# Tile 24 of w_down in nine transfers of 64 to 2 partitions instead of one of 128

## The chip, the core and the metric

The kernel runs on one core of one Trainium2 chip. The metric is device time in microseconds (us), one launch of the whole program, the median of three runs. A lower number is better. Beside the times there is one profiled execution, whose trace is read in what follows.

## The reference

One token (`x`, 1024 numbers) goes through a decoder layer whose two branches run in parallel, and both are added to `x`:

```
xn = layernorm(x)
q  = xn @ wq                                 # 1024 x 4096
p  = softmax(q k^T / sqrt(128))              # the last 4096 keys, 4 key heads, 32 query heads
a  = (p v) @ wo                              # 4096 x 1024
h  = gelu(xn @ w_gate) * (xn @ w_up)         # 1024 x 3584 each
y  = x + a + h @ w_down                      # 3584 x 1024
```

All of it is float32. With a single token every weight and every cached key and value is read once and used for one multiply-add per number, so the kernel moves 94.4 MB from HBM to do matrix-vector products.

## The kernel before

All large inputs pass through one buffer, `ring`, of 176 KB on each of the 128 partitions. A table `pieces` lists what is loaded, in order, and where in the ring: wq in two pieces, the keys, values, w_gate and w_up in two each, wo in two, and w_down in eight. The function `pump` issues the transfer of the next piece as soon as its place in the ring is no longer in use, and `done` frees a place when the last instruction that reads the piece has been recorded. All these transfers are issued by SyncE (SP), through the helper `dma` (line 219 of the profile), so SP's queue has them in the order of the table, and SP waits there for the engines that still read the old piece.

w_down has 3584 rows. Partition p holds rows 28p to 28p+27, and tile t is the row 28p+t of every partition: 128 partitions by 1024 numbers, 4 KB on each partition, 512 KB in all. The eight pieces are the tiles 0 to 11, 12 to 19, 20 and 21, 22 and 23, and then 24, 25, 26 and 27 one by one. Tile 27 comes in two transfers of half its columns.

The last part of the program multiplies these tiles by the hidden vector `hz`. Some tiles go to VectorE (DVE, `multiply_add`, line 213), which keeps a sum per partition in `part`; the others go to TensorE (PE, line 158). At the very end the order is: tiles 20 to 23, then tile 24 on PE (into `sums`), then the fold of DVE's `part` on PE, then tile 25 on PE, an addition on DVE (`x_out`, line 189), tile 26 and the two halves of tile 27 on PE (into `acc`), and after each half an addition on DVE into `y` and two stores to HBM (`out_y`), one from SP and one from ScalarE.

Waits are found by a small recorder, the class `Program`. It notes which bytes each operation reads and writes. Every transfer has a lane of its own, that is a semaphore of its own, which has counted 16 when the transfer is complete (`op["rank"] = 16`). A compute instruction that reads a piece waits for 16 on that semaphore; PE's first matmul of tile 24 is one of them.

Of the kernel before, what the change touches and what calls it, by code (L numbers as in the profile page):

```python
# [24 lines left out]

RING = 176 * KB
SCRATCH = 1024
HEADS_A = [0, 2, 4, 6, 8, 10, 12, 14]
HEADS_B = [0, 2, 4, 6, 8, 10, 12, 14]
HID_A = [0, 2, 4, 6, 8]  # L30
# [5 lines left out]
class Program:  # L36

    def __init__(self, nc):  # L40
        self.nc = nc
        self.ops = []
        self.seen = {}
        self.engines = dict(pe=nc.tensor, dve=nc.vector, act=nc.scalar, pool=nc.gpsimd, sp=nc.sync)

    @staticmethod
# [5 lines left out]
        hi = lo + 1 + sum(abs(s) * (n - 1) for s, n in ap.ap[1:])  # L52
        return ap.tensor.name, p0, p0 + count, lo, hi

    def add(self, engine, emit, reads, writes, dma=False, tag=None):
        op = dict(engine=engine, emit=emit, dma=dma, needs={}, tag=tag, id=len(self.ops),
                  boxes=[self.box(a) for a in writes + reads])
        op["lane"] = f"dma{op['id']}" if dma else engine
        for writing, aps in ((False, reads), (True, writes)):
            for ap in aps:  # L60
                name, p0, p1, lo, hi = self.box(ap)
                for wrote, q0, q1, a, b, other in self.seen.get(name, ()):
                    if not (writing or wrote) or q0 >= p1 or p0 >= q1 or a >= hi or lo >= b:
                        continue
                    if other["lane"] == op["lane"] and (engine == "pe" or not wrote):
                        continue
                    lane = other["lane"]
                    op["needs"][lane] = max(op["needs"].get(lane, -1), other["id"])
        for writing, aps in ((False, reads), (True, writes)):
            for ap in aps:  # L70
                name, p0, p1, lo, hi = self.box(ap)
                kept = self.seen.setdefault(name, [])
                if writing:
                    kept[:] = [
                        k for k in kept
                        if not (p0 <= k[1] and k[2] <= p1 and lo <= k[3] and k[4] <= hi)
                    ]
                kept.append((writing, p0, p1, lo, hi, op))
        self.ops.append(op)
        return op  # L80

    def plan(self):
        known = {e: {} for e in self.engines}
        for op in self.ops:
            mine = known[op["engine"]]
            waits = []
            for lane, other in sorted(op["needs"].items(), key=lambda n: -n[1]):
                if mine.get(lane, -1) >= other:
                    continue
                waits.append(other)  # L90
                for k, v in self.ops[other]["after"].items():
                    mine[k] = max(mine.get(k, -1), v)
            op["waits"] = waits
            op["after"] = dict(mine)
            op["after"][op["lane"]] = op["id"]
        for op in self.ops:
            for other in op["waits"]:
                self.ops[other]["told"] = True
        counts = {}
        for op in self.ops:  # L100
            if op["dma"]:
                op["rank"] = 16
            elif op.get("told"):
                counts[op["engine"]] = counts.get(op["engine"], 0) + 1
                op["rank"] = counts[op["engine"]]
# [41 lines left out]
def decode_layer(nc, x, k_cache, v_cache, wq, wo, w_gate, w_up, w_down, out):  # L147
# [29 lines left out]
    def dve(call, reads, writes, engine="dve"):  # L177
        prog.add(engine, call, reads, writes)
# [9 lines left out]
    def add(o, a, b):  # L188
        dve(lambda e: e.tensor_add(o, a, b), [a, b], [o])  # L189
# [24 lines left out]
            [i, factor, other], [o],  # L214
        )

    def dma(engine, o, i, reads=(), writes=(), tag=None):
        return prog.add(
            engine, lambda e: e.dma_start(o, i), list(reads), list(writes), dma=True, tag=tag  # L219
        )  # L220

    ring = sbuf("ring", P, RING)
# [2 lines left out]
    def rows(w, a):  # L225
        return w[512 * a:512 * (a + 1), :].rearrange("(p r) n -> p (r n)", r=4)

    def heads_of(a):
        return wo[2048 * a:2048 * (a + 1), :].rearrange("(p t) n -> p (t n)", p=P)

    hidden_rows = w_down.rearrange("(p t) n -> p t n", p=P)
# [12 lines left out]
    def load(kind, i, at, size):  # L244
        slot = ring[:, at * KB:(at + size) * KB]
        held[kind, i] = slot
        if kind == "v":
            src = v_cache[0, 2 * i:2 * i + 2, SK - WIN:, :].rearrange("g (p j) d -> p g (j d)", p=P)
            dma("sp", slot.rearrange("p (g n) -> p g n", g=2), src, writes=[slot], tag=(kind, i))
        elif kind == "k":  # L250
            src = k_cache[0, 2 * i:2 * i + 2, SK - WIN:, :].rearrange("g (s j) d -> s g (j d)", g=2, j=64)
            dma("sp", slot, src, writes=[slot], tag=(kind, i))
        elif kind == "d":
            lo, hi = i
            halves = 2 if lo == TD - 1 else 1
            wide = slot.rearrange("p (t n) -> p t n", n=D)
            for half in range(halves):
                cols = slice(half * D // halves, (half + 1) * D // halves)
                dst = wide[:, :, cols]
                dma("sp", dst, hidden_rows[:, lo:hi, cols], writes=[dst], tag=(kind, i, half))  # L260
        else:
            src = {
                "q": lambda: rows(wq, i), "g": lambda: rows(w_gate, i), "u": lambda: rows(w_up, i),
                "o": lambda: heads_of(i),
            }[kind]()
            dma("sp", slot, src, writes=[slot], tag=(kind, i))
# [4 lines left out]
    def pump():  # L271
        while queue:
            kind, i, at, size = queue[0]
            if any(at < hi and lo < at + size for lo, hi in live.values()):
                return
            load(*queue.pop(0))
            live[kind, i] = (at, at + size)
# [12 lines left out]
    for k in range(2):  # L290
        dst = x_out[31 + 64 * k:33 + 64 * k, :, :]
# [316 lines left out]
    def head(t):  # L608
        return oz[:, 32 * t:32 * t + 64]
# [38 lines left out]
    def contract(kind, i, z, dve_tiles, rows):  # L648
        w = held[kind, i].rearrange("p (t n) -> p t n", n=D)
        count = w.shape[1]  # L650
        rest = [(z(t), w[:, t, :]) for t in range(count) if t not in dve_tiles]
        if rows:
            tiles_on_rows(rest)
        else:
            for pair in rest:
                tile_on_pe(*pair)
        for t in dve_tiles:
            tile_on_dve(z(t), w[:, t, :])
        done(kind, i)
# [38 lines left out]

    state["total"] = 2 * TO + 12 - len(HEADS_A + HEADS_B + HID_A)
    contract("o", 0, head, HEADS_A, True)  # L700
    contract("o", 1, lambda t: head(TO + t), HEADS_B, True)
    contract("d", (0, 12), column, HID_A, True)
    add(out_part, acc[:].rearrange("p a n -> p (a n)"), out_part)
    contract("d", (12, 20), lambda t: column(12 + t), HID_B, False)
    contract("d", (20, 22), lambda t: column(20 + t), HID_C, False)
    contract("d", (22, 24), lambda t: column(22 + t), HID_D, False)
    tile_on_pe(column(24), held["d", (24, 25)])
    tile_on_pe(unit[:], out_part)
    tile_on_pe(column(25), held["d", (25, 26)], True)
    add(x_out[:].rearrange("p f n -> p (f n)"), sums[:], x_out[:].rearrange("p f n -> p (f n)"))  # L710
    for half in range(2):
        half_on_pe(column(26), held["d", (26, 27)], half, True, False)
    stores = out.rearrange("a b (f c n) -> (a b) f c n", f=2, c=4)
    for half in range(2):
        half_on_pe(column(27), held["d", (27, 28)], half, False, True)
        add(y[:, half, :], acc[:, half, :P], x_out[:, half, :])
        for k, engine in enumerate(("sp", "act")):
            src = y[31 + 64 * k:33 + 64 * k, half, :]
            dma(
                engine, stores[0, half, 2 * k:2 * k + 2, :], src, reads=[src],  # L720
                tag=("out", half, k),
            )
# [25 lines left out]
```

## Time and profile before

| | |
|---|---|
| median of 3 runs | 226.78 us (226.62 to 226.94) |
| the profiled execution's own time | 226.83 us |
| its span in the trace | 225.5 us |
| bytes read from HBM | 94.38 MB, 419 GB/s over the span |
| DMA busy | 9 tenths or more of the 16 engines' time in nearly every fortieth of the span |
| DVE, PE, ACT busy | 64%, 39%, 12% of the span |

A busy share of DMA is the mean over the core's 16 DMA engines: 0.25 in a stretch can be four engines that work through it while twelve are idle. The share can lie a little over 1, since a packet's record overlaps the next one's. The chain of waits is the path that ended last, followed back from the last instruction. A wait for a transfer is shown there from its issue to its landing, so it contains the time in which the transfer stood behind earlier ones.

### The profile page before, as it was taken

The numbers are of one execution on the slowest core, as the hardware profiler recorded it, in microseconds if no ns is written. First come the engines' busy times: TensorE is split into PE (matmuls) and PEld (weight loads), VectorE is DVE, ScalarE is ACT, GpSimd is POOL, SyncE is SP. The second block draws the span as 40 slices with busy tenths as digits, with TensorE's granted clock in tenths as the row PEclk, the third lists the DMA queues.
The fourth block names the chain that finished last, engine by engine and source line by source line (L and its number), as shares of the span: only waits on it lengthen the run. The fifth ranks groups of instructions, "written<-read, shape, count | busy, mean of one in ns | idle before, by whom it ended". The sixth has DMA issues, their size and how long they took to land.

```text
span 225.5 us, 1396 instructions
## 1 busy us (share of the span) xinstructions
PE 87.5 (39%) x574; PEld 34.8 (15%) x574; DVE 143.2 (64%) x127; ACT 26.3 (12%) x45; POOL 0.7 (0%) x6
## 2 busy tenths in 40 slices
PE   1200000007699007989002537137339204408475
PEld 0100000006263002462000111011002001002131
DVE  7500998499727990000998699869538804938691
ACT  2000000004555001482000300200000000000000
POOL 1000000000000000000000000000000000000000
PEclk9999999999999755999755667857855855965889
DMA  9899899899989999999999998999999999999992
GB/s 373 372 395 535 372 395 535 349 405 478 468 349 426 465 401 503 427 397 471 427 397 392 433 509 387 478 391 491 419 395 488 419 395 413 427 439 442 382 405 111
DMA packets 3317, 94.46 MB, mean 419 GB/s; under 512 B 350, under 2 KB 366, under 8 KB 1008
## 3 DMA queue, kind: packets, MB, share of 16 engines
q1 hardware_dynamic: 3288, 94.38, 97.5%
q8 instruction: 4, 0.07, 0.1%
q10 hardware_dynamic: 24, 0.01, 0.0%
q14 instruction: 1, 0.01, 0.0%
HBM read 94.38 MB, written 0.00 MB: 419 GB/s over the span
## 4 chain that ended last, share of the span: by engine, by line
DMA 65%; DVE 26%; PE 7%; issue 1%; SPq 1%; DVEq 0%
DVE part L213 24%; DMA ring<-in_B_w_down 19%; DMA ring<-in_A_wq 18%; DMA ring<-in_B_w_gate 15%; DMA ring<-in_A_wo 13%; PE acc L158 3%; PE tp L163 2%; PE s_p L158 2%; DVE part L209 1%; SPq L219 1%; DVE rows_sb L186 0%; DVE part L189 0%; DVEq L118 0%; SPq L118 0%
## 5 line engine op out<-in xcount | busy, mean ns | idle before, releaser
L213 DVE SCALAR_TENSOR_TENSOR part<-ring,xz,part 128x3584 f32<-128x3584 f32 (+1 forms) x19 | 78.8, 4148 | 26.6 <-DMA ring<-in_B_w_gate 22.6
L163 PE MATMUL tp<-ident,ring 128*128 128x128 f32 x128 | 20.3, 303 | 44.4 <-DMA ring<-in_A_k_cache 42.8
L213 DVE SCALAR_TENSOR_TENSOR part<-ring,oz,part 128x1024 f32<-128x1024 f32 x15 | 19.3, 1285 | 9.9 <-DMA ring<-in_A_wo 9.4
L172 ACT ACTIVATE ring<-tp 128x512 f32<-128x512 f32 x32 | 18.1, 596 | 58.4 <-PE tp L163 58.0
L163 PEld LDWEIGHTS tp<-ident,ring 128*128 128x128 f32 x128 | 15.0, 152 | 51.2 <-DMA ring<-in_A_k_cache 42.9
L209 DVE TENSOR_SCALAR part<-ring,xz 128x3584 f32<-128x3584 f32 (+1 forms) x3 | 6.5, 2176 | 19.7 <-DMA ring<-in_A_wq 12.1
L158 PE MATMUL acc<-ring,oz 128*32 128x512 f32 x64 | 11.7, 899 | 16.8 <-DMA ring<-in_A_wo 16.8
L213 DVE SCALAR_TENSOR_TENSOR part<-ring,hz,part 128x1024 f32<-128x1024 f32 x10 | 12.8, 1285 | 6.1 <-DMA ring<-in_B_w_down 5.8
L158 PE MATMUL acc<-part,unit 128*32 128x448 f32 (+1 forms) x48 | 7.3, 742 | 22.3 <-DVE part L213 22.3
L158 PE MATMUL o_p<-ring,pT 128*32 128x512 f32 x64 | 11.0, 847 | 7.1 <-DMA ring<-in_A_v_cache 6.5
L158 PE MATMUL acc<-ring,hz 128*32 128x128 f32 (+1 forms) x60 | 8.0, 616 | 10.1 <-DMA ring<-in_B_w_down 10.1
L158 PE MATMUL s_p<-ring,qz 128*32 128x512 f32 x64 | 9.3, 598 | 0.0
L163 PE MATMUL tp<-ident,rows_sb 128*128 128x128 f32 x16 | 3.5, 361 | 12.0 <-ACT rows_sb L172 11.8
L158 PE MATMUL sums<-ring,hz 128*32 128x256 f32 x72 | 6.2, 482 | 4.7 <-DMA ring<-in_B_w_down 4.7
L158 PEld LDWEIGHTS acc<-ring,oz 128*32 128x32 f32 x64 | 2.5, 155 | 26.6 <-DMA ring<-in_A_wo 19.4
L158 PEld LDWEIGHTS acc<-part,unit 128*32 128x32 f32 x48 | 1.4, 126 | 26.4 <-DVE part L213 24.2
L172 ACT ACTIVATE rows_sb<-s_p,negm 128x512 f32<-128x512 f32 x2 | 1.4, 687 | 30.4 <-DVE negm L209 30.4
L158 PEld LDWEIGHTS o_p<-ring,pT 128*32 128x32 f32 x64 | 2.6, 149 | 14.5 <-issue 13.4
L158 PE MATMUL acc<-ring,xz 128*32 128x448 f32 x32 | 4.8, 767 | 0.0
L158 PEld LDWEIGHTS acc<-ring,hz 128*32 128x32 f32 x60 | 2.2, 135 | 15.8 <-issue 14.0
L163 PEld LDWEIGHTS tp<-ident,rows_sb 128*128 128x128 f32 x16 | 2.3, 179 | 15.5 <-ACT rows_sb L172 13.6
L158 PEld LDWEIGHTS sums<-ring,hz 128*32 128x32 f32 x72 | 2.4, 136 | 9.2 <-DMA ring<-in_B_w_down 7.3
(85 smaller groups left out, 47.8 us busy)
## 6 DMA issues: line engine op xcount, KB each, us to landing
ring<-in_B_w_gate SPq DMA_DIRECT2D x2, 7168.0 KB, 31.9
ring<-in_B_w_up SPq DMA_DIRECT2D x2, 7168.0 KB, 33.9
ring<-in_A_k_cache SPq DMA_DIRECT2D x2, 4096.0 KB, 39.7
ring<-in_A_v_cache SPq DMA_DIRECT2D x2, 4096.0 KB, 34.8
ring<-in_B_w_down SPq DMA_DIRECT2D x1, 6144.0 KB, 42.9
ring<-in_B_w_down SPq DMA_DIRECT2D x1, 4096.0 KB, 38.8
ring<-in_B_w_down SPq DMA_DIRECT2D x2, 1024.0 KB, 40.4
ring<-in_B_w_down SPq DMA_DIRECT2D x3, 512.0 KB, 42.0
```

What stands on the lines that cost most here:

```text
L158: "pe", lambda e: e.matmul(o, lhsT, rhs, start=start, stop=stop),
L163: prog.add("pe", lambda e: e.transpose(o, i, eye), [i, eye], [o])
L172: "act", lambda e: e.activation(o, i, func, scale=scale, **kw),
L209: dve(lambda e: e.tensor_scalar(o, i, s1, s2, op0=op0, **kw), reads, [o])
L213: lambda e: e.scalar_tensor_tensor(o, i, factor, other, op0=ALU.mult, op1=ALU.add),
L219: engine, lambda e: e.dma_start(o, i), list(reads), list(writes), dma=True, tag=tag
```

## The change

Tile 24 alone is loaded in another way. In place of one transfer of 128 partitions there are nine, of 64, 39, 5, 5, 5, 3, 3, 2 and 2 partitions, one after the other down the partitions. Each partition still receives its 4 KB of the same bytes at the same place. The nine share one lane and so one semaphore: `group` names the lane, each transfer adds 16 to `sizes`, and whoever waits for the tile waits for 9 x 16 = 144. Nothing else in the program is different.

```diff
+UNEVEN = 24
+SHARES = [64, 39, 5, 5, 5, 3, 3, 2, 2]
...
-    def add(self, engine, emit, reads, writes, dma=False, tag=None):
+    def add(self, engine, emit, reads, writes, dma=False, tag=None, group=None):
...
-        op["lane"] = f"dma{op['id']}" if dma else engine
+        op["lane"] = engine
+        if dma:
+            first = self.groups.setdefault(group, op["id"]) if group else op["id"]
+            op["lane"] = f"dma{first}"
+            self.sizes[op["lane"]] = self.sizes.get(op["lane"], 0) + 16
...
-                op["rank"] = 16
+                op["rank"] = self.sizes[op["lane"]]
...
             lo, hi = i
+            if lo == UNEVEN:
+                at = 0
+                for count in SHARES:
+                    some = slice(at, at + count)
+                    at += count
+                    dst = slot[some, :]
+                    dma("sp", dst, hidden_rows[some, lo, :], writes=[dst], tag=(kind, i), group=(kind, i))
+                return
             halves = 2 if lo == TD - 1 else 1
```

SP's queue is the place where instructions move. Its end before the change, with tiles 20 to 27 as the transfers of 128 partitions by 2048 (two tiles), 1024 (one tile) and 512 numbers (half a tile), and what each waits for:

```order
14 L219 DMA ring<-in_B_w_down 128x2048 [waits s_pe,s_dve] x2
15 L219 DMA ring<-in_B_w_down 128x1024 [waits s_dve]
16 L219 DMA ring<-in_B_w_down 128x1024 [waits s_pe]
17 L219 DMA ring<-in_B_w_down 128x1024 [waits s_dve]
18 L219 DMA ring<-in_B_w_down 128x512
19 L219 DMA ring<-in_B_w_down 128x512 [waits s_pe]
20 L219 DMA out_y<-part 2x128 [waits s_dve] x2
```

The same place in the changed program (its lines are eight further down):

```order
14 L227 DMA ring<-in_B_w_down 128x2048 [waits s_pe,s_dve] x2
15 L227 DMA ring<-in_B_w_down 64x1024 [waits s_dve]
16 L227 DMA ring<-in_B_w_down 39x1024
17 L227 DMA ring<-in_B_w_down 5x1024 x3
18 L227 DMA ring<-in_B_w_down 3x1024 x2
19 L227 DMA ring<-in_B_w_down 2x1024 x2
20 L227 DMA ring<-in_B_w_down 128x1024 [waits s_pe]
21 L227 DMA ring<-in_B_w_down 128x1024 [waits s_dve]
22 L227 DMA ring<-in_B_w_down 128x512
23 L227 DMA ring<-in_B_w_down 128x512 [waits s_pe]
```

One row has become nine, and the transfers of tiles 25, 26 and 27 stand eight places later in SP's queue. The wait that tile 24 had is now on the first of the nine, and the other eight wait for nothing.

More of the change, by code (lines that the diff above doesn't have):

```diff
@@ L43, in __init__ @@
         self.seen = {}
+        self.groups, self.sizes = {}, {}
         self.engines = dict(pe=nc.tensor, dve=nc.vector, act=nc.scalar, pool=nc.gpsimd, sp=nc.sync)
@@ L215, in multiply_add, with dma @@
         )
-    def dma(engine, o, i, reads=(), writes=(), tag=None):
+    def dma(engine, o, i, reads=(), writes=(), tag=None, group=None):
         return prog.add(
-            engine, lambda e: e.dma_start(o, i), list(reads), list(writes), dma=True, tag=tag
+            engine, lambda e: e.dma_start(o, i), list(reads), list(writes), dma=True, tag=tag,
+            group=group,
         )
```

## The prediction

> **What bounds the kernel now.** I read the page's chain and DMA sections first, then the chain in order of time, then PE's last 10 us, then a table of quarter microseconds over the end. The page:
>
> ```profile
> span 225.5 us, 1396 instructions
> DMA 65%; DVE 26%; PE 7%; issue 1%; SPq 1%; DVEq 0%
> DMA packets 3317, 94.46 MB, mean 419 GB/s; under 512 B 350, under 2 KB 366, under 8 KB 1008
> q8 instruction: 4, 0.07, 0.1%
> q10 hardware_dynamic: 24, 0.01, 0.0%
> HBM read 94.38 MB, written 0.00 MB: 419 GB/s over the span
> ```
>
> The bytes bound it: 94.38 MB at 419 GB/s are the 225 us. Sixteen DMA engines share this, so one brings 26.2 GB/s, and 4 KB (one partition's row of a tile) take it 0.156 us. The chain shows what the end hangs on:
>
> ```profile
> 180.50 42.73 DMA ring<-in_B_w_down
> 223.28 0.47 PE acc L158 x8
> 223.77 0.29 DVE part L189
> ```
>
> The last half of tile 27 lands at 223.23. From there it is 2.27 us to the end of the span (0.47 of PE, 0.29 of DVE, then the stores), and 1.33 us more from the span, 225.5, to the execution's own time, 226.83; that is 0.05 above the median of 226.78. Whatever moves the landing moves the time. PE's rows at the end show that it follows the landings:
>
> ```profile
> 218.22 0.64 PE L158 MATMUL sums<-ring,hz 128*32 128x256 f32 x8 [0.71 <-DMA ring<-in_B_w_down]
> 219.49 0.64 PE L158 MATMUL sums<-ring,hz 128*32 128x256 f32 x8 [0.62 <-DMA ring<-in_B_w_down]
> 219.94 0.62 PE L158 MATMUL sums<-part,unit 128*32 128x256 f32 x8
> 220.78 0.64 PE L158 MATMUL sums<-ring,hz 128*32 128x256 f32 x8 [0.21 <-DMA ring<-in_B_w_down]
> 222.03 1.04 PE L158 MATMUL acc<-ring,hz 128*32 128x128 f32 x24 [0.61 <-DMA ring<-in_B_w_down]
> 223.28 0.43 PE L158 MATMUL acc<-ring,hz 128*32 128x128 f32 x8 [0.21 <-DMA ring<-in_B_w_down]
> ```
>
> Tile 24 starts at 219.49, tile 25 at 220.78, tile 26 at 222.03, the last half of 27 at 223.28: a tile takes 1.25 to 1.29 us, 8 rows on each of 16 engines, so a row costs 0.157 us, in agreement with the page's mean. Now the end, where the last column but one is the mean busy share of the 16 engines:
>
> ```profile
> 220.50:220.75 0.25, 0.06 (x4) 0.00 (x0) 0.00 (x0) 0.00 (x0) 0.00 (x0) 1.00 1.08 410
> 220.75:221.00 0.25, 0.22 (x4) 0.16 (x8) 0.00 (x0) 0.00 (x0) 0.00 (x0) 1.00 0.71 262
> 221.00:221.25 0.25, 0.25 (x8) 0.00 (x0) 0.00 (x0) 0.00 (x0) 0.00 (x0) 1.00 0.56 213
> 221.25:221.50 0.25, 0.17 (x4) 0.00 (x0) 0.01 (x1) 0.00 (x0) 0.00 (x0) 1.00 0.40 156
> 221.50:221.75 0.25, 0.00 (x0) 0.00 (x0) 0.25 (x1) 0.00 (x0) 0.00 (x0) 1.00 0.32 123
> 221.75:222.00 0.25, 0.00 (x0) 0.00 (x0) 0.16 (x1) 0.00 (x0) 0.00 (x0) 1.00 0.32 123
> 222.00:222.25 0.25, 0.22 (x8) 0.22 (x12) 0.00 (x0) 0.00 (x0) 0.00 (x0) 1.00 0.24 90
> 222.25:222.50 0.25, 0.25 (x16) 0.15 (x8) 0.00 (x0) 0.00 (x0) 0.00 (x0) 1.00 0.15 57
> 222.50:222.75 0.25, 0.25 (x12) 0.11 (x8) 0.00 (x0) 0.00 (x0) 0.00 (x0) 1.00 0.09 33
> 222.75:223.00 0.25, 0.25 (x8) 0.05 (x7) 0.00 (x0) 0.00 (x0) 0.00 (x0) 1.00 0.00 0
> ```
>
> Times 16 the share counts engines: all until 220.75, about 9 at 221.0 to 221.25, 5 until 222.0, 4 until 222.25, then 2.4, 1.4 and none. So the engines do not end together. An early half ends near 221.0, and four run on past 222.0, of which the last ends at about 222.8, another near 222.65, two near 222.3 (beyond 222.0 the three shares hold 0.48 x 0.25 x 16 = 1.9 us of work; these ends give 0.8 + 0.65 + 0.3 + 0.3 = 2.05). From 220.75 on the eight shares sum to 2.79, times 0.25 that is 0.70 us if all had shared it: a perfect balance ends at 221.45, 1.35 us earlier. That is the most any deal of rows can bring. Four late engines and four instruction packets (q8) of some 16 KB, each of which occupies one engine, fit together; I take these as the cause.
>
> **The change, part by part.** It does not change bytes; it deals the 128 rows of tile 24 otherwise. How many engines does a transfer use? The page's 350 packets under 512 B answer it for two sizes: 21 loads of 128 partitions with 16 closing packets each and 7 small transfers (3 loads of x, 4 stores) with 2 each make 336 + 14 = 350. So 128 rows went to 16 engines and 2 rows to 2. For 64, 39, 5 and 3 no row exists. I take equal shares over as many engines as divide the count: 64 to 16 engines by 4, 39 to 13 by 3, 5 to 5, 3 to 3, and all of them starting with the same first engine.
>
> [...]
>
> Rows per engine are then 14, 14, 12, 10, 10 on the first five (numbered 0 to 4), 7 on each of 5 to 12, and 4 on each of 13 to 15, where each had 8. In time at 0.157 us: +0.94 on engines 0 and 1, +0.63 on 2, +0.31 on 3 and 4, -0.16 on eight, -0.63 on three. Each transfer also closes on its engine; a tile in one transfer (1.25) against two halves (2 x 0.64, from 222.64 to 223.28) bounds a closing from above by 0.03, and eight more on engine 0 by 0.24; I take 0.1, from nothing to 0.24.
>
> An early engine that gets six rows ends at 221.0 + 0.94 + 0.1 = 222.04, still before 222.8. So what counts is where the late ones sit, and no view gives an engine its number. If the last is among the middle eight it ends at 222.64: 0.16 us gained. If the late three are 13 to 15, the last ends at 222.17, the fourth at 222.3 - 0.16 = 222.14: 0.63 gained. If it sits on 2 to 4: 0.31 to 0.63 lost. That the three shares then meet near 222.1 is arithmetic and says nothing of the places.
>
> The issues. Eight more stand in SP's queue behind tile 24's wait, and the transfers of tiles 25 to 27 behind these; PE waits for those, and at the end DVE.
>
> ```profile
> 160.55 30.84 SPq L219 DMA_DIRECT2D ring<-in_B_w_down  x9
> L219 SPq DMA_DIRECT2D ring<-in_B_w_down x9: 328/328/10887, 160.6 to 180.5; - x9
> DMA to landing us min/median/max: 34.2/41.6/42.9
> ```
>
> Eight issues of 0.33 us are 2.6 us on SP near 180, and they are hidden: a landing comes 42 us after its issue, as each transfer stands in line behind the earlier ones. Without that cover it would be 2.6 us of delay. One issue took 10.9 us, the last one, until 160.55 + 30.84 = 191.39. No engine's wait explains that; I read it as a queue that was full (about nine transfers of 8 rows and a closing packet). In the change engine 0 has 14 more entries to hold (6 rows, 8 closings). It frees them as it works: six or seven more rows of tiles 0 to 11 (48 KB each, 1.8 us), then about seven of tiles 12 to 19 (1.2 us), so SP is done near 211. The data it issues last are fetched from 220.8 on. It stays hidden by some 10 us, so I take 0; it would cost something only if the queue drained 10 us later than I work out.
>
> The wait for 144 in place of 16 costs nothing by itself: one wait instruction before, one now. If tile 24 landed late, the fold and tile 25 on PE would stand behind it. PE itself allows earlier landings: tile 25 can start when the fold is done (220.56), and 0.64, 0.61, 0.43 and 0.47 us of work from there end at 222.7, where they now end at 223.75, so up to 1.0 us of gain would get through.
>
> There is one more cost without a row: what two engines do that write into neighbouring partitions at the same time. All big loads here spread over 128 partitions at once. The first of the nine fills only partitions 0 to 63, with all 16 engines, the other eight only 64 to 127. If 64 neighbouring partitions take data at no more than half the full rate, tile 24 takes 2 x 1.25 = 2.5 us for engines that go in step: +1.25. Below, it is nothing, since the engines are up to 2 us out of step and one's wait is the other's free way; above, +1.25 and 0.94 on the front engines, 2.2. I take nothing for my forecast, because the tail shows engines out of step by more than one tile's time, and keep 1.25 as a rival.
>
> [...]
>
> Sum for the forecast: -0.16 (last engine in the middle) + up to 0.1 (closings, small waits) + 0 (issues) + 0 (wait) = -0.1 us, 226.7.
>
> **The rivals.**
>
> 1. *The late engines are the last three.* 0.63 gained, 226.2. For it: the packet records show the two engines of the small x loads in the early pack, so the late ones are not quite at the front; the instruction packets are the only large extra load. Against: nothing ties them to the back, and by count only 3 of the 14 other places are there.
> 2. *Half of the partitions take half the rate.* The engines of the early pack, nine of which end within half a microsecond of each other, fill partitions 0 to 63 together and then 64 to 127 together; in the pieces of 5, 3 and 2 partitions they write to direct neighbours. It decides as soon as two engines in step share a way in; price 1.25 (0.6 to 2.2), 228.0. For it: the early pack is in step. Against: the late four are not, and they set the end.
> 3. *The late engine is one of 2 to 4.* It gets 2 to 4 rows more: 0.31 to 0.63 lost, 227.1 to 227.4.
> 4. *The change does not do what it says*: 39 does not split, and one engine takes all 39 rows. Engine 0 then has 4 + 39 + 3 + 2 + 2 = 50 rows, 42 more, 6.6 us, from 221.0 to 227.6, 4.8 after the end now: 231.6.
>
> **How the numbers follow.** Of 16 places, 0 and 1 are out; of the other 14 the middle eight hold the last engine with 0.57, the back three and 2 to 4 with 0.21 each. Rival 2 I give 0.26 and rival 4 0.02, which leaves 0.72: by count 0.41, 0.155 and 0.155. I move a little from the middle and some from 2 to 4 to the back, as a judgement (if the front pair is spared, its neighbours may be too): forecast 0.37, rival 1 0.25, rival 3 0.10, rivals 2 and 4 as said. A measurement of this kernel tells 0.2%, 0.45 us, from no change. The forecast is within it; rival 1 is faster; rivals 2, 3 (0.09 of 0.10) and 4 are slower. So faster 0.25, same 0.38, slower 0.37. Rival 1 lies at 226.2 with closings and landing to either side, rival 2 with most of its chance below 228.3. The range 226.05 to 228.3 leaves out the rest: rival 4 with 0.02, the upper part of rival 2 with 0.08, and 0.05 below. The forecast's own range is 226.4 to 227.2.
>
> **What would show it.** In the quarter microseconds at the end of the changed kernel: right, if the shares fall as before and the last engine ends within 0.3 us of 222.8. If three or four engines end together near 222.15 and the share stays near 0.5 until then, rival 1. If the GB/s around tile 24 (218 to 222) fall clearly below 400 while the share stays at 1, rival 2; the share would then be high for longer and PE's start of tile 24 come after 220.5. A tail of one or two engines past 223 without such a fall is rival 3, one engine past 226 rival 4. SP's last issue should end near 211; if it ends after 220, my cover of the issues is gone. What would make the prediction wrong most likely is the place of the late engines, which I could only count.

## The result, and the profile after

| | before | after |
|---|---|---|
| median | 226.7 us (226.6 to 226.94, 5 runs) | 229.15 us (229.05 to 229.37, 5 runs) |
| ratio, 95% interval | | 1.0109 (1.0094 to 1.0124) |
| span of the profiled execution | 225.5 us | 228.0 us |

The change makes the kernel 2.45 us slower. The forecast was 226.7 with a range up to 228.3, so the time lies outside. The page of the changed kernel first, the span and the packets:

```profile
span 228.0 us, 1404 instructions
DMA packets 3355, 94.46 MB, mean 414 GB/s; under 512 B 388, under 2 KB 404, under 8 KB 1046
```

The same bytes come at 414 GB/s in place of 419. The packets under 512 B are 38 more than the 350 before. One transfer of 16 closing packets has gone, so the nine have 54: 16 + 13 + 3 x 5 + 2 x 3 + 2 x 2. That count fits a split over 16, 13, 5, 3 and 2 engines, as the prediction assumed. The trace's packet records (start, duration and size of every packet) fit the same first engine too: followed from the end of one packet to the start of the next, those of tiles 20 to 27 can be put into 16 chains with none left over, of which two bring 14 rows of tile 24, one 12, two 10, eight 7 and three 4. Some other deals fit them as well, but not one in which each transfer starts on the engine behind the last one's. Now the stretch in which tile 24 comes in, microsecond by microsecond; the last two columns are the busy share of the 16 engines and the GB/s. Before the change:

```profile
216.00:217.00 1.00, 1.00 (x24) 0.48 (x18) 1.00 (x1) 0.00 (x0) 0.00 (x0) 0.86 1.07 426
217.00:218.00 1.00, 0.52 (x12) 0.04 (x4) 0.96 (x2) 0.00 (x0) 0.00 (x0) 1.00 0.96 381
218.00:219.00 1.00, 0.64 (x8) 0.16 (x8) 0.96 (x2) 0.00 (x0) 0.00 (x0) 1.00 1.03 414
219.00:220.00 1.00, 0.51 (x12) 0.23 (x16) 0.87 (x1) 0.00 (x0) 0.00 (x0) 1.00 1.01 399
```

and after it:

```profile
215.00:216.00 1.00, 1.00 (x16) 0.52 (x12) 0.96 (x2) 0.00 (x0) 0.00 (x0) 0.50 0.92 377
216.00:217.00 1.00, 1.00 (x16) 0.44 (x12) 1.00 (x1) 0.00 (x0) 0.00 (x0) 0.50 1.24 242
217.00:218.00 1.00, 1.00 (x13) 0.39 (x8) 0.96 (x2) 0.00 (x0) 0.00 (x0) 0.50 0.97 176
218.00:219.00 1.00, 0.65 (x8) 0.00 (x0) 0.60 (x1) 0.00 (x0) 0.00 (x0) 0.50 0.98 197
219.00:220.00 1.00, 0.00 (x0) 0.00 (x0) 0.00 (x0) 0.00 (x0) 0.00 (x0) 1.00 0.97 205
220.00:221.00 1.00, 0.23 (x4) 0.16 (x8) 0.18 (x1) 0.00 (x0) 0.00 (x0) 1.00 1.08 250
221.00:222.00 1.00, 0.40 (x8) 0.00 (x0) 1.00 (x1) 0.00 (x0) 0.00 (x0) 1.00 0.95 328
222.00:223.00 1.00, 0.94 (x12) 0.50 (x16) 0.10 (x1) 0.00 (x0) 0.00 (x0) 0.71 1.00 389
```

The engines are as busy as before (a share of 1.03 over the six rows from 216 to 222) and bring half as much. A packet's whole time is counted in the stretch in which it starts, so one microsecond can show 1.24 and the next 0.97. For six microseconds the six rows average 233 GB/s, where the four of before average 405: 6 x (405 - 233) = 1.03 MB are missing, and at 405 GB/s those are 2.5 us. That is as much as the whole loss. The stretch brings 1.4 MB, and tile 24 is 0.52 MB of it, so tiles that were not changed are slowed with it. The packet records show this one by one: before the change none of the 256 packets of 8 KB of tiles 20 to 23 takes more than 0.33 us; after it the last 15 of them, which start while tile 24 is coming in, take 0.60 to 0.81 us. PE's rows show the same:

```profile
220.76 0.64 PE L166 MATMUL sums<-ring,hz 128*32 128x256 f32 x8 [2.12 <-DMA ring<-in_B_w_down]
222.06 0.79 PE L166 MATMUL sums<-ring,hz 128*32 128x256 f32 x8 [0.66 <-DMA ring<-in_B_w_down]
222.61 1.10 PE L166 MATMUL sums<-part,unit 128*32 128x256 f32 x8
223.46 1.10 PE L166 MATMUL sums<-ring,hz 128*32 128x256 f32 x8
224.39 1.75 PE L166 MATMUL acc<-ring,hz 128*32 128x128 f32 x32
```

The first row is tile 22, which PE multiplies while DVE has tile 23. Their transfer was not touched, and PE starts on it at 220.76 in place of 218.22, already 2.54 us late. Tile 24 starts at 222.06 in place of 219.49, 2.57 late. Nothing further is lost behind it. So the late engines, still bringing tiles 22 and 23, are held up while the early ones are in tile 24. The chain of waits ends with PE now:

```profile
181.50 40.51 DMA ring<-in_B_w_down
222.02 0.04 issue
222.06 2.50 PE sums L166 x24
224.56 1.38 PE acc L166 x24
225.94 0.02 issue
225.97 0.55 DVE part L197 x2
```

After tile 24 PE works through until 225.94, at a granted clock of 0.50 for most of it. The landings end so shortly before that both give nearly this end. PE's last weight load still waits for one, and the engines' share ends at 225.25:

```profile
225.66 0.21 PEld L166 LDWEIGHTS acc<-ring,hz 128*32 128x32 f32 x8 [0.21 <-DMA ring<-in_B_w_down]
224.75:225.00 0.25, 0.25 (x12) 0.23 (x8) 0.25 (x1) 0.00 (x0) 0.00 (x0) 0.50 0.09 33
225.00:225.25 0.25, 0.25 (x13) 0.21 (x8) 0.03 (x1) 0.00 (x0) 0.00 (x0) 0.50 0.04 16
```

By the packet records the last packet of tile 27 ends at 225.16 in place of 222.81, 2.35 us later, and the span is 2.5 us longer. So the transfers account for nearly all of the loss, and PE's lower clock for 0.2 us at most. SP's queue was no part of it:

```profile
174.42 34.13 SPq L227 DMA_DIRECT2D ring<-in_B_w_down  x16
```

Its last issue ended at 174.42 + 34.13 = 208.55, more than ten microseconds before the last tile's data were fetched.

### The profile page after: what moved, and what is told of

Same layout as the page of the kernel before. It is cut to its first block, busy times and chain, and to the rows that moved or that the text cites. A ratio compares the mean times of both kernels' runs of the same rounds, so it can differ in the third digit from the quotient of the medians.

```text
span 228.0 us, 1404 instructions
## 1 busy us (share of the span) xinstructions
PE 89.2 (39%) x574; PEld 35.8 (16%) x574; DVE 143.1 (63%) x127; ACT 26.3 (12%) x45; POOL 0.7 (0%) x6
## 4 chain that ended last, share of the span: by engine, by line
DMA 63%; DVE 25%; PE 8%; SPq 1%; issue 1%; DVEq 0%
DVE part L221 23%; DMA ring<-in_A_wq 18%; DMA ring<-in_B_w_down 18%; DMA ring<-in_B_w_gate 15%; DMA ring<-in_A_wo 13%; PE acc L166 3%; PE tp L171 2%; PE s_p L166 2%; SPq L227 1%; DVE part L217 1%; PE sums L166 1%; DVE rows_sb L194 0%; DVE part L197 0%; DVEq L126 0%; SPq L126 0%
## 5 line engine op out<-in xcount | busy, mean ns | idle before, releaser
L166 PE MATMUL acc<-ring,oz 128*32 128x512 f32 x64 | 11.0, 850 | 17.5 <-DMA ring<-in_A_wo 17.5
L166 PE MATMUL o_p<-ring,pT 128*32 128x512 f32 x64 | 11.8, 905 | 7.7 <-DMA ring<-in_A_v_cache 7.0
L166 PE MATMUL sums<-ring,hz 128*32 128x256 f32 x72 | 7.9, 586 | 6.3 <-DMA ring<-in_B_w_down 6.3
L166 PEld LDWEIGHTS acc<-ring,hz 128*32 128x32 f32 x60 | 2.7, 159 | 15.4 <-issue 14.4
```

Source lines behind the costliest of these rows:

```text
L166: "pe", lambda e: e.matmul(o, lhsT, rhs, start=start, stop=stop),
```

## The experiments

Three theories were set against each other. N: engines that write into neighbouring partitions at the same time share a way in, and 64 neighbouring partitions take data at about half the rate. D: the uneven deal of rows puts the front engines late. T: each further transfer costs something. In all experiments the kernel before ran beside them on the same chip.

| run | what is loaded in another way | median, us | ratio to before, 95% interval |
|---|---|---|---|
| e1 | tile 24: partitions 0-63, 64-127 | 230.19 | 1.0148 (1.0133 to 1.0163) |
| e2 | tile 24: four times 256 columns | 226.92 | 1.0007 (0.9997 to 1.0017) |
| e3 | tile 24: 64, 48, 16 neighbours | 229.99 | 1.0140 (1.0125 to 1.0155) |
| e7 | tile 24: 64, 39, 25 neighbours | 229.57 | 1.0122 (1.0107 to 1.0137) |
| e4 | tiles 0-11: partitions 0-63, 64-127 | 245.15 | 1.0810 (1.0773 to 1.0847) |
| e5 | tiles 0-11: source near, target spread | 226.90 | 1.0004 (0.9992 to 1.0015) |
| e6 | tiles 0-11: source spread, target near | 245.61 | 1.0831 (1.0799 to 1.0862) |
| e9 | tiles 0-11: even, odd partitions | 226.70 | 0.9997 (0.9986 to 1.0008) |
| e10 | tile 24: even, odd partitions | 226.74 | 1.0001 (0.9992 to 1.0010) |
| e11 | tile 24: the change's deal, spread | 227.31 | 1.0022 (1.0013 to 1.0031) |
| e15 | tile 24: 64, 52, 6, 6, spread | 228.15 | 1.0058 (1.0043 to 1.0073) |
| e12 | 24 KB more on each of 2 engines | 226.74 | 0.9998 (0.9988 to 1.0007) |
| e13 | 24 KB more on each of 5 engines | 226.84 | 1.0004 (0.9995 to 1.0014) |
| e14 | 24 KB more on each of 8 engines | 227.54 | 1.0034 (1.0023 to 1.0046) |

### Neighbours, deal, or number of transfers: e1, e2, e3, e7

```diff
-SHARES = [64, 39, 5, 5, 5, 3, 3, 2, 2]
+SHARES = [64, 64]                     # e1
+SHARES = [64, 48, 16]                 # e3
+SHARES = [64, 39, 25]                 # e7
+SHARES = [256, 256, 256, 256]         # e2, as columns: slot[:, some], hidden_rows[:, lo, some]
```

> Tile 24 in two transfers, partitions 0 to 63 and 64 to 127. Each of the 16 engines still has 8 rows (4 and 4). Theory N (engines that write into neighbouring partitions at the same time share a way in, and 64 partitions take data at about half the rate): tile 24 takes up to 2.5 us in place of 1.25, so +0.6 to +1.3 us, with about 200 GB/s at a busy share of 1 while it loads. Theory D (the uneven deal of rows puts the front engines late): 0. Theory T (each further transfer costs, 2.45 us for eight more, 0.31 each): +0.3.

> Tile 24 in four transfers of all 128 partitions and 256 columns each, sharing one semaphore. Rows per engine and partitions in reach stay as before the change, only the number of transfers grows by three (and packets have 1 KB). N: 0, at most +0.1 for the smaller packets. D: 0. T: +0.9.

> Tile 24 in three transfers of 64, 48 and 16 neighbouring partitions. Every engine has 4 + 3 + 1 = 8 rows as before, so the deal is even, but each transfer fills neighbouring partitions. N: slower, +1.0 to +1.8 us (4 rows at half rate, 3 at half or a little better, 1 at a quarter). D: 0. T: +0.6.

> Tile 24 in transfers of 64, 39 and 25 partitions: about the deal of the change (12 rows on engines 0 to 4, 7 on 5 to 12, 4 on 13 to 15), without the pieces of 5, 3 and 2 partitions in which up to five engines write to direct neighbours. N: +1.2 to +1.8 us, less than the change's 2.45 by what the small pieces cost. D: nearly the change's loss less two rows on engines 0 and 1, about +2. T: +0.6.

Measured: +3.4, +0.2 (not clear of zero), +3.2 and +2.8 us. The rows for 216 to 220 us, of e1:

```profile
216.00:220.00 4.00, 2.61 (x28) 0.81 (x20) 2.52 (x2) 0.00 (x0) 0.00 (x0) 0.64 1.04 207
```

of e3:

```profile
216.00:220.00 4.00, 2.41 (x24) 0.79 (x16) 2.33 (x2) 0.00 (x0) 0.00 (x0) 0.65 1.03 203
```

and of e2:

```profile
216.00:220.00 4.00, 3.41 (x42) 1.32 (x38) 3.85 (x3) 0.00 (x0) 0.00 (x0) 0.66 1.05 387
```

D falls as the cause: e1 and e3 leave every engine its eight rows, by an equal split like the one that the changed kernel's packets fit, and lose more than the change does. T falls too: four transfers over all partitions cost 0.2 us (0.4 at the upper end of the interval), two over halves 3.4. N is right in kind, with about 205 GB/s at a full share, but its sizes were too small for each of the three. PE has half its clock at the end of e1, e3 and e7 (a granted 0.50 from 223 to 225 us). Two rows of e1 and the end of its chain of waits:

```profile
223.00 1.08 PE L166 MATMUL sums<-ring,hz 128*32 128x256 f32 x8 [1.67 <-DMA ring<-in_B_w_down]
223.86 1.08 PE L166 MATMUL sums<-part,unit 128*32 128x256 f32 x8
181.12 45.39 DMA ring<-in_B_w_down
226.52 0.04 issue
226.56 0.47 PE acc L166 x8
```

A piece that took PE 0.64 us takes 1.08. Yet the chain ends with the last landing, at 226.52 in place of 223.23, so e1's loss is the transfers'. By the packet records the last packet ends 3.3 us later than before in e1, 2.8 in e3 and 2.7 in e7, which is nearly each one's loss. Why the finer and uneven deals lose less than two halves is not shown.

### The rate in a long stretch, and which side it is: e4, e5, e6, e9

The change is taken out and the piece of tiles 0 to 11 (6 MB) is split in two instead:

```diff
+if lo == 0:
+    for at in (0, 64):                                                     # e4
+        dma("sp", wide[at:at + 64], hidden_rows[at:at + 64, lo:hi, :], ...)
+    for h in range(2):                                                     # e5
+        src = w_down[1792 * h:1792 * (h + 1), :].rearrange("(p t) n -> p t n", p=P)
+        dma("sp", wide[:, 6 * h:6 * h + 6, :], src[:, 0:6, :], ...)
+        dma("sp", wide[64 * h:64 * h + 64], hidden_rows[h:P:2, lo:hi, :], ...)   # e6
+        dma("sp", wide[h:P:2], hidden_rows[h:P:2, lo:hi, :], ...)                # e9
```

> The change is taken out (tile 24 in one transfer). Instead the piece of tiles 0 to 11 (6 MB, 48 KB on each partition) comes in two transfers, partitions 0 to 63 and 64 to 127, on one semaphore; each engine has 4 + 4 rows. It measures the rate into 64 partitions in a long stretch. Theory N at the target: half rate, 6 MB take 29 us in place of 14.5, so +12 to +14.5 us, with about 210 GB/s at a busy share near 1 between 186 and 215 us. If it were the source in HBM (rows of half the matrix only): the same. If neighbouring partitions cost nothing: 0 (within 0.5).

> The piece of tiles 0 to 11 in two transfers of 128 partitions, tiles 0 to 5 and 6 to 11 of the buffer, each read from one half of w_down (rows 0 to 1791, rows 1792 to 3583). So the source is near together and the target is spread. Other rows of w_down than the reference's are read, so the output is another. N at the target: 0 (within 0.5 us). If the source makes it slow: +12 or more, like e4.

> The piece of tiles 0 to 11 in two transfers into partitions 0 to 63 and 64 to 127, read from the even rows p of the matrix and then the odd ones. So the target is near together and the source is spread over the whole matrix as before. The rows meet other hidden values than in the reference, so the output is another. N at the target: +12 to +14.5 us, as e4. If the source makes it slow: 0.

> The piece of tiles 0 to 11 in two transfers, the even partitions and then the odd ones, each spread over all 128 in steps of two; 4 + 4 rows for each engine. If what counts is only how many of the partitions' ways in a transfer reaches: 0 to +1. If what counts is whether two engines are at the same one at the same time (each engine takes 4 rows that follow each other, 8 partitions of the 128, two engines can still meet): anything up to e4's +14.

Measured: +18.4, +0.1, +18.8 and -0.1 us (e5 and e9 not clear of zero). One row each for the thirty microseconds from 189 on, of the kernel before:

```profile
189.00:219.00 30.00, 16.70 (x116) 4.74 (x116) 23.48 (x19) 0.00 (x0) 0.00 (x0) 0.72 0.97 414
```

of e4:

```profile
189.00:219.00 30.00, 5.40 (x32) 1.24 (x32) 10.28 (x8) 0.00 (x0) 0.00 (x0) 0.61 0.98 203
```

of e5:

```profile
189.00:219.00 30.00, 16.53 (x116) 4.79 (x116) 23.34 (x19) 0.00 (x0) 0.00 (x0) 0.69 1.00 423
```

of e6:

```profile
189.00:219.00 30.00, 6.14 (x32) 1.31 (x32) 10.28 (x8) 0.00 (x0) 0.00 (x0) 0.56 0.98 203
```

and of e9:

```profile
189.00:219.00 30.00, 16.90 (x116) 4.87 (x116) 23.45 (x19) 0.00 (x0) 0.00 (x0) 0.71 0.97 412
```

It is the target: 64 neighbouring partitions take 203 GB/s, wherever the rows come from (e4, e6), while 128 partitions take 423 with each transfer's rows from one half of the matrix (e5), and 64 in steps of two take 412 (e9). The ratio of e4 to the kernel before is 0.49. That engines share a way in to neighbouring partitions is N's explanation and no run shows it; what the rows show is the rate. The loss of 18.4 us is more than the 12 to 14.5 expected. The piece has 6.29 million bytes, 31 us at 203 GB/s and 15.2 at 414, so 15.8 us of it are this piece. The rest stands in front of it in the queue. PE's starts on the second half of wo, which was not changed, and on tiles 0 to 11, before:

```profile
189.00 5.29 PE L158 MATMUL acc<-ring,oz 128*32 128x512 f32 x32 [12.93 <-DMA ring<-in_A_wo]
203.63 6.50 PE L158 MATMUL acc<-ring,hz 128*32 128x512 f32 x28 [9.33 <-DMA ring<-in_B_w_down]
```

and in e4:

```profile
192.15 5.40 PE L166 MATMUL acc<-ring,oz 128*32 128x512 f32 x32 [16.05 <-DMA ring<-in_A_wo]
222.54 5.56 PE L166 MATMUL acc<-ring,hz 128*32 128x512 f32 x28 [24.99 <-DMA ring<-in_B_w_down]
```

PE starts on wo 3.15 us late and on tiles 0 to 11 18.9 late. By the packet records the last four 64 KB packets of wo take 4.6 to 5.1 us in place of 2.4. At the last half of tile 27 the delay is still 18.7 us (241.97 in place of 223.28), so nothing further is lost behind.

### The same deal, with the partitions spread: e10, e11, e15

```diff
-SHARES = [64, 39, 5, 5, 5, 3, 3, 2, 2]
+SHARES = [(0, 2, 64), (1, 2, 64)]                                # e10: first, step, count
+SHARES = [(0, 2, 64), (25, 2, 39), (1, 4, 5), (3, 4, 5), (103, 4, 5),
+          (105, 4, 3), (117, 4, 3), (21, 2, 2), (123, 4, 2)]     # e11
+SHARES = [(0, 2, 64), (13, 2, 52), (1, 2, 6), (117, 2, 6)]       # e15
-dst = slot[some, :]
+dst = slot[first:first + step * (count - 1) + 1:step, :]         # and the same rows of w_down
```

> Tile 24 in two transfers, the 64 even partitions and the 64 odd ones; 4 + 4 rows for each engine, as with the two neighbouring halves, which cost 3.4 us. If neighbouring partitions are the cause, steps of two take it away: 0 (within 0.3). If any transfer of 64 partitions is slow here: +3.

> The change's deal of rows to engines without its neighbouring blocks: nine transfers of 64, 39, 5, 5, 5, 3, 3, 2 and 2 partitions, but the 64 are the even partitions, the 39 the odd ones from 25 to 101, and the small ones stand four partitions apart at the two ends. Rows per engine are 14, 14, 12, 10, 10, seven each on eight, four on three, as in the change. Theory E (an engine's own time sets when it ends, so rows taken from a late engine help): -0.16 if the last engine is among the middle eight, -0.63 if the late three are the last three, +0.3 to +0.6 if it is one of engines 2 to 4. Theory W (what counts is the way in to a partition, which gets the same bytes whoever brings them): 0 to +0.3. If the small transfers and not the neighbouring blocks were the cost: +1 to +2.5.

> Tile 24 in four spread transfers: the 64 even partitions, 52 odd ones from 13 to 115, and two of 6 odd ones at the ends. Rows per engine: 10 on engines 0 to 5, 8 on 6 to 12, 4 on 13 to 15. Theory E with the late three at the back: -0.4 to -0.6. With the last engine among 6 to 12: 0. Among 0 to 5: +0.3. Theory W (a way in takes the same bytes whoever brings them): 0. If transfers with fewer than 16 engines crowd even when spread: +0.3 to +0.8, with GB/s below 350 between 217 and 219 us.

Measured: 0.0 (not clear of zero), +0.5 and +1.3 us. The row for 216 to 220 us, of e10:

```profile
216.00:220.00 4.00, 2.69 (x44) 1.02 (x40) 3.71 (x3) 0.00 (x0) 0.00 (x0) 0.97 1.01 400
```

of e11:

```profile
216.00:220.00 4.00, 3.35 (x32) 0.99 (x24) 3.67 (x3) 0.00 (x0) 0.00 (x0) 0.61 1.02 321
```

and of e15:

```profile
216.00:220.00 4.00, 2.36 (x36) 0.76 (x28) 3.47 (x3) 0.00 (x0) 0.00 (x0) 0.92 1.03 314
```

The very deal of the change costs 0.5 us in place of 2.45 when its partitions are spread. So most of the loss, four fifths, was the neighbours. The rest looks the same in the rows, fewer GB/s at a full share: e10, with 64 partitions in both of its transfers, keeps 400 GB/s, while e11 and e15, with further transfers of 52, 39, 6, 5, 3 or 2, fall to 321 and 314. A spread set of partitions is not enough there; which engine meets which at which partition no view shows, and this stays open. No version gained anything, and none beats the kernel before.

### Where the late engines sit: e12, e13, e14

The change is taken out; one more transfer of k partitions stands between tiles 26 and 27 and is waited for with tile 26:

```diff
+("z", k, 64, 24),                                # k = 2, 5, 8, between tiles 26 and 27
+dma("sp", slot[0:4 * k:4, :], hidden_rows[0:4 * k:4, 0:6, :].rearrange("p t n -> p (t n)"), ...)
```

> The change is taken out. One more transfer stands between tiles 26 and 27: 24 KB (six rows) into each of 2 partitions, 0 and 4, read from w_down a second time and used by nothing; PE's first matmul of tile 26 waits for it too. It puts 6 x 0.157 = 0.94 us on engines 0 and 1 alone. An early engine (end near 221.0) takes it without moving the end (222.8): 0. If a late engine is one of the two: +0.9. The working of the prediction says 0.

> The same with 5 partitions (0, 4, 8, 12, 16): 0.94 us more on engines 0 to 4. If one of the four late engines is among 0 to 4 (rival 3's place): +0.4 to +0.9. If not: 0, at most +0.1.

> The same with 8 partitions (0 to 28 in steps of four): 0.94 us more on engines 0 to 7. If the last engine is among 0 to 7: +0.9; if only the third or fourth of the late ones: +0.4 to +0.5; if all four are among 8 to 15: 0, at most +0.2.

Measured: 0.0, +0.1 (neither clear of zero) and +0.8 us. The packets under 512 B are 355 in e13 and 358 in e14, five and eight more than the 350 before, so the added transfers close on five and on eight engines. That five engines do carry more in e13 is seen in its quarter microseconds:

```profile
221.25:221.50 0.25, 0.08 (x4) 0.00 (x0) 0.10 (x1) 0.00 (x0) 0.00 (x0) 1.00 0.64 246
221.50:221.75 0.25, 0.00 (x0) 0.00 (x0) 0.25 (x1) 0.00 (x0) 0.00 (x0) 1.00 0.60 229
222.50:222.75 0.25, 0.25 (x12) 0.16 (x8) 0.00 (x0) 0.00 (x0) 0.00 (x0) 1.00 0.11 41
222.75:223.00 0.25, 0.25 (x8) 0.00 (x0) 0.00 (x0) 0.00 (x0) 0.00 (x0) 1.00 0.00 0
```

The share between 221.25 and 221.75 is 0.62, where it was 0.36 before: four more engines at work. But the end is at 222.75 as it was. In e14 it is not:

```profile
222.75:223.00 0.25, 0.25 (x10) 0.25 (x13) 0.00 (x0) 0.00 (x0) 0.00 (x0) 1.00 0.19 74
223.00:223.25 0.25, 0.25 (x16) 0.12 (x7) 0.00 (x0) 0.00 (x0) 0.00 (x0) 1.00 0.15 57
223.25:223.50 0.25, 0.25 (x13) 0.14 (x8) 0.00 (x0) 0.00 (x0) 0.00 (x0) 1.00 0.09 33
```

One or two engines now run on to 223.5. Engines 0 to k-1 are read here as those that a transfer of k partitions uses: the changed kernel's packet records fit one first engine for all transfers, and the numbers of the engines are in no view. So no engine of 0 to 4 is late enough to matter, and at least one of 5 to 7 is one of the last: 0.94 us of extra load moved the end by about 0.75. The packet records, in which the added packets are the only ones of 24 KB, say more. In e13 four of the five start within 0.2 us of each other and one 0.8 behind. In e14 five of the eight start within 0.4 us and three 1.0 to 1.4 behind the fifth. So at least two of the late engines are among 5 to 7. What makes these engines late was not tested; the prediction's four instruction packets stay a guess.

## Why the prediction was wrong

- **What bounds the kernel: right.** The bytes bound it, the landings of the last tiles set the end, and the 2.5 us of missing bytes came out as 2.45 us of time.
- **The split of the transfers: right.** 388 packets agree with 16, 13, 5, 3 and 2 engines; rival 4 is excluded. That all transfers start with the same first engine was an assumption when it was made, and the forecast's -0.16 us rests on it; the changed kernel's packet records fit the deal of 14, 14, 12, 10, 10, 7 and 4 rows.
- **Six more rows on an early engine cost nothing: right.** e12 and e13 put just that on the front engines and show 0.0 and +0.1 us.
- **The place of the late engines: right as counted.** At least two of the late four sit among 5 to 7, in the middle eight; that the very last one does is not shown. Rival 3 is excluded by e13, and rival 1, which needed the late three at the back, by e14. The most that this deal could then have brought is the forecast's 0.16 us.
- **The issues: right.** They were hidden; SP's last issue ended at 208.55, near the 211 worked out from a full queue.
- **The neighbouring partitions: wrong, and this is the step that failed.** The prediction took "nothing for my forecast", because the engines are up to 2 us out of step and "one's wait is the other's free way". The rate is in fact 203 in place of 414 GB/s (e4), and being out of step does not spare the engines from it. The late engines' transfers of tiles 22 and 23 were slowed by the early ones in tile 24, and PE's start on them came 2.54 us late.
- **Rival 2 named the effect and its sign** (GB/s clearly below 400 at a share of 1, PE's start of tile 24 after 220.5: 205 GB/s for 216 to 220, and 222.06), **but its price of 1.25 us was too low by half.** It counted tile 24's 0.52 MB alone at half rate. The slow stretch held 1.4 MB, nearly three times that. So the range, built on this price, ended at 228.3, 0.85 us too low, and even the upper price of 2.2 would have fallen short.

The chance was wrong in the same way as the price. The tail's rows did show the engines out of step, but no row showed that this spares them.

## What to carry to other kernels

Look at which partitions each transfer fills, not only at how many engines carry it: a split into neighbouring blocks halved the rate at a full busy share (203 against 414 GB/s over 30 us, e4), and in the changed kernel it slowed the transfers in front of it and behind it too (8 KB packets of tiles 22 and 23 took 0.60 to 0.81 us in place of 0.31, and the 4 KB packets that start between 220 and 221 us, most of them of the tiles behind, 0.24 to 0.35 in place of 0.16). A low GB/s beside a DMA share of 1 is the sign, and here a split by columns or by even and odd partitions cost nothing clear of noise (e2, e10) where two halves cost 3.4 us (e1). Before dealing work away from a late engine, find it by adding a small transfer of k partitions near the end and watching whether the end moves (0.1 us with k = 5, 0.8 with k = 8 here).

## What the runs showed of the hardware that was not expected

- 64 partitions in steps of two load at the full rate, 412 GB/s over 30 us, against 203 for 64 neighbours (e9, e4).
- Spread partitions did not keep the rate where most of the transfers had 52 partitions or fewer: 321 and 314 GB/s against 400 with 64 and 64 (e11, e15, e10).
- The slow transfers hold up what is in flight around them: packets of the untouched tiles took 0.60 to 0.81 us in place of 0.31 in the changed kernel, and the last of wo's 4.6 to 5.1 in place of 2.4 in e4.
- PE was granted a clock of 0.50 in the last pieces of the changed kernel (224.75 to 225.25) and took 1.08 us for e1's pieces of 0.64. It cost little there, and e12, where PE's pieces from 218.21 on took 1.08 us too, lost nothing.
- An issue on SP can stand for long. No view shows what it waits for; as in the prediction, I read it as a full queue. The changed kernel's issues have 253, 328 and 18288 ns as their shortest, median and longest:

```profile
L227 SPq DMA_DIRECT2D ring<-in_B_w_down x17: 253/328/18288, 160.1 to 201.0; - x17
```
